# Moving value loads, mixing matrices, a pair of exponentials and row splits in a talking-heads attention with two expert layers

## The chip, the cores and the metric

The kernel runs on one core of a Trainium2 chip. The metric is the device time of one execution in microseconds (us). TensorE (PE) multiplies, VectorE (DVE), ScalarE (ACT) and GpSimd (POOL) work on tiles in SBUF and PSUM, and SyncE (SP) issues the DMAs named here.

## The reference, cut to what matters

```python
def _attn_ref(q, k, v, w_pre, w_post):            # (4, 12, 448, 64)
    scores = scale * np.matmul(q, k.transpose(0, 1, 3, 2))
    scores = np.einsum('bhij,hg->bgij', scores, w_pre)
    scores = scores - np.max(scores, axis=-1, keepdims=True)
    attn = np.exp(scores)
    attn = attn / (np.sum(attn, axis=-1, keepdims=True) + 1e-09)
    attn = np.einsum('bhij,hg->bgij', attn, w_post)
    return np.matmul(attn, v)

def _moe_ref(x, w_in, w_out):                     # x (1792, 768), w_in (768, 2048)
    h = x @ w_in
    g = np.where(h > 0.0, h, np.exp(np.minimum(h, 0.0)) - 1.0)
    return g @ w_out
```

A third layer routes each row of the result to one of eight experts (`x + gate * (relu(x @ w1) @ w2)`, or `x` alone where a skip score is not positive). The change doesn't touch it.

## The kernel before, in words

**Attention.** The 4 batches have 448 query rows each, cut into 4 tiles of 120, 120, 120 and 88 rows, so there are 16 tiles. A tile is worked on in three *periods* of four blocks of 10 query rows (the last tile of a batch has fewer), 48 periods in all, and a period in two *units* of two blocks. The heads are mixed by a matrix product, for which the 12 heads x 10 rows of a block have to lie on the partitions. The scores come out of TensorE with the rows on the partitions (`qk`, L154), ScalarE and VectorE move them from PSUM into one large tile `s` per attention tile (L158, L159), and a DMA per block brings them into a buffer `d` in the other layout (`relayout`, L193). There are two such tiles `s`, used in turn, and eight buffers `d`.

A period n, in the program's order: SP issues the relayout of the second unit of period n+1, the stores of results, and the query and key loads of period n+7. Then, for each of the two units: the first mixing `c` (`mix_pre`, L206, with the matrices `kpre_low` and `kpre_up`); after the first unit's, the relayout of the first unit of period n+2; the second mixing `f` of a unit of period n-1 (`mix_post`, L252); the row maxima `nmx` (`top`, L215, VectorE); two copies of `f` into `at` (L258, one on ScalarE, one on VectorE); and the exponentials `e` (`softmax`, L224, two on ScalarE). After the second unit's exponentials are issued, TensorE computes two heads' pairs of scores for period n+5 (`qk`). Then come the norms (`norm`, L231, L232 on VectorE and L236 on GpSimd), the score moves, the split of queries, and the product of `at` of the previous tile with the values (`av`, L274) and its copy (L283). The PSUM pool `ps_w` has five buffers, shared by `c` and `qk`.

**The order.** Engines run their instructions in the order in which the program issues them; up to the routing tables this order is written by hand. Only behind the point where the tables are made is the order of instructions chosen by a scheduler.

**Start.** Before the first period the program loads queries, keys, the two mixing weights and the 12 pieces of values of batch 0 (`load_v`, L125, on SP), computes all scores of tile 0, issues the relayouts of period 0, builds the mixing matrices (`kron`, L307 and L303 copy them on VectorE, L309 and L311 mask them on GpSimd, DMAs at L357, L359 and L366 put them into their tiles `kpre_low`, `kpre_up` and `kpost`), and issues four pairs of scores of tile 1. Values of the later batches are loaded right after their predecessors' last use, in `av`.

**The second layer.** It starts beside the last five periods of the attention and is a generator, resumed by `next(mix)`. Rows `xr` are loaded (`load_x`, L511), and split into a high part (ScalarE, L515) and a low part (L519, on POOL and VectorE in turn). A weight is loaded as 64-bit words, narrowed to 32 bits (`narrow`: L488 on ScalarE, L491 to L498 on VectorE, and a merge at L500 on POOL), and split in the same way (L463, L464). Six pieces of rows and one weight make one group of products (`products`, L585), 18 matrix multiplications. The groups go through the weights and the four row tiles: weight 0 with row tiles 0, 1, 2, then weight 1 with row tiles 0, 1, 2, then both with row tile 3. The elementwise step follows (`elu`, L592 to L595), and `g` is stored. The second product `o` (L859) reads stored rows back (`gr`, L732) and narrowed weights `wr` (L805).

## Time and profile before

| | us |
|---|---|
| median of 3 runs | 1108.67 |
| lowest and highest run | 1106.9, 1115.65 |
| the profiled execution | 1108.77 |
| its span (first to last instruction) | 1107.0 |
| PE busy | 1024.1 |
| DVE, ACT, POOL busy | 802.3, 566.7, 390.7 |

The span leaves out 1.77 us around it. TensorE's mean granted clock in the profiled execution was 0.981 of full speed. Of the span's 1107.0 us TensorE is busy for 93%. Busy time of other engines matters only where TensorE waits for them.

### The profile page before, as it was taken

How to read it: one execution, taken by the hardware profiler on the slowest of the kernel's cores; microseconds unless marked ns; L12 is line 12 of the kernel's file. 1: busy time of each engine (PE TensorE's matmuls, PEld its weight loads, DVE VectorE, ACT ScalarE, POOL GpSimd, SP SyncE). 2: the span in 40 equal slices, each digit the busy share in tenths (PEclk: the TensorE clock that was granted, in tenths of full speed). 3: DMA queues.
4: the chain of work that ended last, by engine and by line, in shares of the span. 5: the costliest groups of instructions: out<-in, count | busy, mean ns of one | idle time of the engine just before them, and what ended most of it. 6: DMA issues, size and time to landing. Idle time of an engine off the chain costs nothing. (4 is left out here: it accounts for less than half of the span.)

```text
span 1107.0 us, 29935 instructions
## 1 busy us (share of the span) xinstructions
PE 1024.1 (93%) x12082; PEld 882.8 (80%) x12082; DVE 802.3 (72%) x1495; ACT 566.7 (51%) x1150; POOL 390.7 (35%) x355
## 2 busy tenths in 40 slices
PE   6998999899899888999999999999999989899997
PEld 4676667666677667899999988999999978788887
DVE  5775777677577668667666557878787856999953
ACT  5664656466465555444544454333333326677751
POOL 2232214123221226232232202535354534756521
PEclk8999999999999999999999999999999998999999
DMA  6453564465455556555566557733333385999800
GB/s 202 170 173 109 164 202 138 131 195 182 110 165 173 166 153 225 171 170 157 193 215 206 178 171 262 237 94 107 96 105 107 94 317 184 392 391 343 328 8 32
DMA packets 134218, 199.67 MB, mean 180 GB/s; under 512 B 35860, under 2 KB 101400, under 8 KB 133821
## 3 DMA queue, kind: packets, MB, share of 16 engines
q1 hardware_dynamic: 131933, 191.27, 52.4%
q0 software_dynamic: 2144, 6.46, 1.6%
q8 instruction: 96, 1.57, 0.6%
q14 instruction: 45, 0.37, 0.1%
HBM read 122.47 MB, written 37.65 MB: 145 GB/s over the span
## 5 line engine op out<-in xcount | busy, mean ns | idle before, releaser
L859 PE MATMUL o<-w,gh 128*128 128x384 f32 (+2 forms) x1344 | 242.5, 339 | 2.9 <-ACT w L463 2.4
L585 PE MATMUL h<-xh,w 128*128 128x448 f32 x1152 | 236.3, 367 | 4.7 <-POOL xh L519 4.7
L859 PEld LDWEIGHTS o<-w,gh 128*128 128x128 f32 x1344 | 234.1, 190 | 7.3 <-ACT w L463 3.6
L585 PEld LDWEIGHTS h<-xh,w 128*128 128x128 f32 x1152 | 216.9, 189 | 23.4 <-POOL xh L519 6.5
L236 POOL TENSOR_SCALAR kr<-kpost,rs 128x60 f32<-128x60 f32 x180 | 77.4, 444 | 284.5 <-DVE rs L232 242.7
L252 PEld LDWEIGHTS f<-kr,e 64*64 64x64 f32 (+2 forms) x5760 | 121.2, 138 | 54.6 <-issue 33.5
L755 DVE SCALAR_TENSOR_TENSOR junk<-x,wrow 128x768 f32<-128x768 f32 x78 | 117.1, 1501 | 40.0 <-ACT x L890 38.6
L252 PE MATMUL f<-kr,e 64*64 64x60 f32 (+2 forms) x5760 | 122.4, 225 | 7.3 <-DVE at L258 1.8
L500 POOL TENSOR_TENSOR wf<-a,p 128x768 f32<-128x768 f32 x32 | 66.6, 2082 | 163.3 <-DVE p L498 122.8
L215 DVE TENSOR_REDUCE nmx<-c 128x1 f32<-128x448 f32 x180 | 104.5, 620 | 25.9 <-PE c L206 25.9
L258 ACT COPY at<-f 128x480 f32<-128x480 f32 x96 | 52.5, 547 | 135.2 <-PE f L252 135.2
L1029 DVE TENSOR_TENSOR wlo<-w1t,whi 128x1536 fp32r<-128x1536 f32 x50 | 111.6, 2255 | 13.6 <-ACT whi L1026 13.6
L224 ACT ACTIVATE e<-c,nmx 128x448 f32<-128x448 f32 x180 | 113.0, 637 | 6.3 <-DVE nmx L215 6.3
L1026 ACT CAST whi<-w1t 128x1536 fp32r<-128x1536 f32 x64 | 94.3, 1483 | 34.1 <-PE ph L1056 17.5
L748 POOL TENSOR_TENSOR prod<-x,wrow 128x768 f32<-128x768 f32 x39 | 93.9, 2434 | 50.0 <-ACT x L890 26.8
L154 PE MATMUL qk<-k,qq 64*120 64x448 f32 (+1 forms) x576 | 90.6, 404 | 17.3 <-ACT e L224 10.3
L206 PE MATMUL c<-d,kpre_up 60*64 60x448 f32 x336 | 85.1, 574 | 11.7 <-ACT s L158 11.7
L274 PE MATMUL xp<-at,v 128*64 128x120 f32 (+3 forms) x1536 | 92.2, 267 | 1.4 <-DVE at L258 1.4
L274 PEld LDWEIGHTS xp<-at,v 128*64 128x64 f32 (+1 forms) x1536 | 75.1, 137 | 21.9 <-issue 17.3
L159 DVE TENSOR_SCALAR s<-qk 120x448 f32<-120x448 f32 (+1 forms) x96 | 58.3, 618 | 45.0 <-PE qk L154 19.8
L206 PE MATMUL c<-d,kpre_low 64*64 64x448 f32 x336 | 84.3, 554 | 3.5 <-DMA kpre_low<-kpre_kr 3.5
L154 PEld LDWEIGHTS qk<-k,qq 64*120 64x120 f32 (+1 forms) x576 | 52.8, 180 | 42.1 <-ACT e L224 25.2
(185 smaller groups left out, 1449.2 us busy)
## 6 DMA issues: line engine op xcount, KB each, us to landing
w1t<-in_moe_w_dram SPq DMA_DIRECT2D x64, 768.0 KB
d<-s SPq DMA_DIRECT2D x168, 210.0 KB
gT<-g SPq DMA_DIRECT2D x64, 224.0 KB
f<-in_moe_w_in_dram SPq DMA_DIRECT2D x16, 768.0 KB
f<-in_moe_w_out_dram SPq DMA_DIRECT2D x16, 768.0 KB
gr<-gT SPq DMA_DIRECT2D x48, 256.0 KB
rk<-in_k_dram SPq DMA_DIRECT2D x24, 224.0 KB
xr<-xT SPq DMA_DIRECT2D x24, 224.0 KB
```

Of the source, the lines that this page charges most:

```text
L154: nc.tensor.matmul(out=ps[:n, :S], lhsT=qt[T, p // 2][rows, a, p % 2, :n], rhs=kt[b, p][rows, z, :], start=(i == 0), stop=(i == 2))
L206: nc.tensor.matmul(out=ps[j * UP:(j + 1) * UP, :S], lhsT=kpre_up[UP:UP + HP, :] if z else kpre_low if len(U) == 2 else kpre[:d[z, j].shape ...
L215: nc.vector.tensor_reduce(out=t, in_=c, op=ALU.max, axis=AX.X, negate=True)
L224: nc.scalar.activation(out=e, in_=c, func=ACTF.Exp, bias=t, accum_out=sms[U][:, i:i + 1])
L252: nc.tensor.matmul(out=ps[to, c // 2, :, z, :], lhsT=e[rows, keys], rhs=kr[rows, :])
L274: nc.tensor.matmul(out=ps[z * 64:(z + 1) * 64, i, :n], lhsT=t[:, z, jc % t.shape[2], :], rhs=att[T][:t.shape[0], jc, 2 * p + z, :n], start ...
L585: nc.tensor.matmul(out=ps, lhsT=w[:, a, kk, :], rhs=xs[tb, kk][:, z, :], start=(kk == 0 and a + z == 0), stop=(kk == NK - 1 and a == 1))
L748: nc.gpsimd.tensor_tensor(out=p[:, :n], in0=x2, in1=w, op=ALU.mult)
L755: nc.vector.scalar_tensor_tensor(out=t[:, o:o + n], in0=x2, scalar=1.0, in1=w, op0=ALU.mult, op1=ALU.mult, accum_out=lg[:, e:e + 1])
L859: mm = nc.tensor.matmul(out=po[c][:, :cols[c].stop - cols[c].start], lhsT=gs[i][fc // GC][:, a, fc % GC, :], rhs=wo[fc][:, z, cols[c]], st ...
L1026: nc.scalar.copy(out=hi, in_=t)
L1029: (nc.vector if dve else nc.gpsimd).tensor_tensor(out=lo, in0=t, in1=hi, op=ALU.subtract)
```

## The change

Four things are moved or resized:

- The loads of values are collected in a list and issued in the period loop, after the relayout and the stores and ahead of the query loads. Those of batch 0 thus stand in period 0, those of a later batch one period after the product that frees their place.
- In the second unit of a period the two exponentials are issued ahead of the two copies of `f`.
- The mixing matrices are built inside the loop over tile 0's scores, when three of its six pairs have been issued, instead of after the loop and the first relayouts.
- The pool `xr` has nine buffers instead of six, and the six splits of row tile 2 are issued in one piece right after the products of row tile 1, ahead of the narrowing of weight 1.

```diff
--- before.py
+++ after.py
@@ -276,7 +276,7 @@
                                              stop=(i == 1 and jc == JC - 1))
             for p in (2 * u, 2 * u + 1):
                 if b + 1 < B and it == len(ROWS) - 1:
-                    load_v(b + 1, p)
+                    values.append((b + 1, p))
 
             def move():
                 x = x_p.tile([128, 2, 120], FP32, tag="x", name="x")
@@ -284,7 +284,7 @@
                 stores.append((xT[b][2 * u:2 * u + 2, :, r0:r0 + n].rearrange("c p n -> p c n"), x[:, :, :n]))
             return move
 
-        stores = []
+        stores, values = [], []
 
         def store():
             for to, x in stores:
@@ -330,8 +330,7 @@
                 split_k(0, 0, nc.vector)
                 load_k(0, 5)
         load_q(1)
-        for p in range(NK):
-            load_v(0, p)
+        values += [(0, p) for p in range(NK)]
         moves = []
         for p in range(NK):
             if p + 1 < NK:
@@ -342,6 +341,22 @@
             if p > 0:
                 moves.pop()()
             moves.append(move)
+            if p == 2:
+                kpre = kron(pre, "kpre", False)
+                kpost = kron(post, "kpost", True)
+
+                kpre_low = const.tile([UP, UP], FP32, name="kpre_low")
+                nc.vector.memset(kpre_low, 0.0)
+                nc.sync.dma_start(out=kpre_low[GAP:, GAP:], in_=kpre[:HP, :HP])
+                kpre_up = const.tile([128, UP], FP32, name="kpre_up")
+                nc.sync.dma_start(out=kpre_up[UP:UP + HP, :], in_=kpre[:HP, :UP])
+                kposts = [const.tile([128, HP], FP32, name=f"kpost{z}") for z in range(2)]
+                for t in kposts:
+                    nc.vector.memset(t, 0.0)
+                nc.vector.tensor_copy(out=kposts[1][:HP].rearrange("p (g i) -> p g i", g=H),
+                                      in_=kpost[:HP].rearrange("p (g i) -> p g i", g=H)[:, :, :HR])
+                for z, first in ((1, UP), (0, GAP), (0, UP + GAP)):
+                    nc.sync.dma_start(out=kposts[z][first:first + HP, :], in_=kposts[1][:HP, :])
         moves.pop()()
         units = [units_of(Gs) for Gs in periods]
         for U in units[0]:
@@ -349,21 +364,6 @@
         load_q(2)
         split_q(1, 0)
         split_q(1, 1)
-        kpre = kron(pre, "kpre", False)
-        kpost = kron(post, "kpost", True)
-
-        kpre_low = const.tile([UP, UP], FP32, name="kpre_low")
-        nc.vector.memset(kpre_low, 0.0)
-        nc.sync.dma_start(out=kpre_low[GAP:, GAP:], in_=kpre[:HP, :HP])
-        kpre_up = const.tile([128, UP], FP32, name="kpre_up")
-        nc.sync.dma_start(out=kpre_up[UP:UP + HP, :], in_=kpre[:HP, :UP])
-        kposts = [const.tile([128, HP], FP32, name=f"kpost{z}") for z in range(2)]
-        for t in kposts:
-            nc.vector.memset(t, 0.0)
-        nc.vector.tensor_copy(out=kposts[1][:HP].rearrange("p (g i) -> p g i", g=H),
-                              in_=kpost[:HP].rearrange("p (g i) -> p g i", g=H)[:, :, :HR])
-        for z, first in ((1, UP), (0, GAP), (0, UP + GAP)):
-            nc.sync.dma_start(out=kposts[z][first:first + HP, :], in_=kposts[1][:HP, :])
         relayout(units[1][0])
         for i in range(4):
             qk(1, i)()
@@ -383,6 +383,8 @@
             late = n >= NP - 5
             if late:
                 next(mix)
+            while values:
+                load_v(*values.pop(0))
             if T2 < len(tiles):
                 if u2 == 0:
                     load_q(T2)
@@ -396,10 +398,13 @@
                     relayout(units[n + 2][0])
                 moves = mix_post(old[i]) if old else []
                 top(cur[i])
+                if i == 1:
+                    softmax(cur[i])
                 if old:
                     moves[1](nc.scalar.copy)
                     moves[0](nc.vector.tensor_copy)
-                softmax(cur[i])
+                if i == 0:
+                    softmax(cur[i])
                 if i == 1 and T < len(tiles):
                     scores = [qk(T, 2 * u), qk(T, 2 * u + 1)]
                 if late:
@@ -469,7 +474,7 @@
         with ExitStack() as ctx:
             f64_p = pool("f64", 2, ctx, side="right")
             cv_p = pool("cv", 1, ctx, side="right")
-            xr_p = pool("xr", 6, ctx, side="right")
+            xr_p = pool("xr", 9, ctx, side="right")
             xh_p = [pool("xh0", NK, ctx, side="right")]
 
             def load_w(src):
@@ -663,13 +668,12 @@
             xh_p.append(pool("xh3", NK, ctx))
             t_p = pool("tables", 1, ctx)
             ps_o = pool("ps_o", 2, space=PSUM)
-            narrowed[1] = narrow(raws.pop(1))
             raws["out"] = load_w_out(0)
             products(1)
-            split_x(2, range(3), both)
+            split_x(2, range(6), both)
+            narrowed[1] = narrow(raws.pop(1))
             elu(1)
             wi[1] = split(narrowed.pop(1), ring_a)
-            split_x(2, range(3, 6), both)
             load_x(3)
             products(2)
             w_jobs(0)
```

The first place is ScalarE in two periods inside a batch. Numbers tell the buffers apart: `f_2541` is the second mixing's result of a first unit, `f_2592` of a second one. Before:

```order
L258 COPY at_2365<-f_2541 128x48x10
L224 ACTIVATE e_2581,sm_2580<-c_2532,nmx_2574 128x448
L224 ACTIVATE e_2583,sm_2580<-c_2533,nmx_2576 128x448
L258 COPY at_2365<-f_2592 128x48x10
L224 ACTIVATE e_2632,sm_2631<-c_2585,nmx_2625 128x448
L224 ACTIVATE e_2634,sm_2631<-c_2586,nmx_2627 128x448
L158 ACTIVATE s_2462<-qk_2636 120x448
L158 ACTIVATE s_2462<-qk_2644 120x448
L141 CAST qq_2670<-rq_2062 128x240
```

The same in the changed kernel:

```order
L258 COPY at_2365<-f_2541 128x48x10
L224 ACTIVATE e_2581,sm_2580<-c_2532,nmx_2574 128x448
L224 ACTIVATE e_2583,sm_2580<-c_2533,nmx_2576 128x448
L224 ACTIVATE e_2630,sm_2629<-c_2585,nmx_2625 128x448
L224 ACTIVATE e_2632,sm_2629<-c_2586,nmx_2627 128x448
L258 COPY at_2365<-f_2592 128x48x10
L158 ACTIVATE s_2462<-qk_2636 120x448
L158 ACTIVATE s_2462<-qk_2644 120x448
L141 CAST qq_2670<-rq_2062 128x240
```

The copy of `f_2592`, which stood between the two pairs of exponentials, stands behind both.

The second place is SP at the start, from the last of the first query loads on (L112, `rq` of 128x720). Before:

```order
L112 DMA rq<-in_q_dram 128x720
L125 DMA v<-in_v_dram 128x384
L125 DMA v<-in_v_dram 64x128
L193 DMA d_154<-s 120x1x448
L193 DMA d_155<-s 120x1x448
L193 DMA d_156<-s 120x1x448
L193 DMA d_157<-s 120x1x448
L112 DMA rq<-in_q_dram 128x720
L357 DMA kpre_low<-kpre_kr 60x60
L359 DMA kpre_up<-kpre_kr 60x64
L366 DMA kpost_330<-kpost_330 60x60
L366 DMA kpost_329<-kpost_330 60x60 x2
```

Ten more rows of value loads stand between the second and the third row there, like the two shown. In the changed kernel:

```order
L112 DMA rq<-in_q_dram 128x720
L350 DMA kpre_low<-kpre_kr 60x60
L352 DMA kpre_up<-kpre_kr 60x64
L359 DMA kpost_253<-kpost_253 60x60
L359 DMA kpost_252<-kpost_253 60x60 x2
L193 DMA d_154<-s 120x1x448
L193 DMA d_155<-s 120x1x448
L193 DMA d_156<-s 120x1x448
L193 DMA d_157<-s 120x1x448
L112 DMA rq<-in_q_dram 128x720
```

Behind that stand the relayouts of period 1, and the values ahead of the relayouts of period 2 (`d_154` and the following, used again):

```order
L193 DMA d_160<-s 120x1x448
L193 DMA d_161<-s 120x1x448
L125 DMA v<-in_v_dram 128x384
L125 DMA v<-in_v_dram 64x128
L193 DMA d_154<-s 120x1x448
L193 DMA d_155<-s 120x1x448
```

The matrices moved ahead of the first relayouts, and the 12 value loads from ahead of the relayouts of period 0 to behind those of period 1.

The third place is SP about the last groups of the first product, where a scheduler chooses the order (`gr` are row loads, `gT` stores of `g`, `wr` weight loads). Before:

```order
L732 DMA gr<-gT_0_65 128x4x128
L596 DMA gT_3_76<-g 128x448
L732 DMA gr<-gT_0_69 128x4x128
L805 DMA wr<-wf_77 128x768
L805 DMA wr<-wf_78 128x768
L805 DMA wr<-wf_79 128x768
L732 DMA gr<-gT_0_73 128x4x128
L732 DMA gr<-gT_0_61 128x4x128
L805 DMA wr<-wf_80 128x768
L805 DMA wr<-wf_81 128x768
L805 DMA wr<-wf_82 128x768
L732 DMA gr<-gT_0_65 128x4x128
```

In the changed kernel:

```order
L601 DMA gT_1_74<-g 128x448
L809 DMA wr<-wf_77 128x768
L736 DMA gr<-gT_0_73 128x4x128
L809 DMA wr<-wf_78 128x768
L601 DMA gT_2_75<-g 128x448
L809 DMA wr<-wf_79 128x768
L736 DMA gr<-gT_0_61 128x4x128
L736 DMA gr<-gT_0_65 128x4x128
L601 DMA gT_3_76<-g 128x448
L736 DMA gr<-gT_0_69 128x4x128
L809 DMA wr<-wf_80 128x768
L736 DMA gr<-gT_0_73 128x4x128
```

The weight loads `wr` are issued further ahead, the first two between stores, and fewer row loads stand ahead of the last three. On PE, the order of the large products is the same.

## Rows read from the trace of the kernel before

**Rows 1.** the page: busy time and share of each engine, then one of the costliest groups.

```profile
PE 1024.1 (93%) x12082; PEld 882.8 (80%) x12082; DVE 802.3 (72%) x1495; ACT 566.7 (51%) x1150; POOL 390.7 (35%) x355
...
L154 PE MATMUL qk<-k,qq 64*120 64x448 f32 (+1 forms) x576 | 90.6, 404 | 17.3 <-ACT e L224 10.3
```

**Rows 2.** PE waits from 60 to 400 us: us in total, times, longest us.

```profile
PE c L206 <- ACT s L158: 11.7, 3, 4.0
PE qk L154 <- ACT e L224: 9.0, 27, 0.4
```

**Rows 3.** timeline of ACT, 120 to 140 us: start, busy, instruction [idle before <-releaser].

```profile
126.60 0.57 ACT L258 COPY at<-f 128x480 f32<-128x480 f32 x1 [0.29 <-PE f L252]
127.06 0.63 ACT L224 ACTIVATE e<-c,nmx 128x448 f32<-128x448 f32 x1
```

**Rows 4.** timeline of VectorE and of PE, 120 to 140 us.

```profile
125.27 1.16 DVE L215 TENSOR_REDUCE nmx<-c 128x1 f32<-128x448 f32 x2
...
127.84 0.88 PE L154 MATMUL qk<-k,qq 64*120 64x448 f32 x5 [0.32 <-ACT e L224]
128.64 1.50 PE L274 MATMUL xp<-at,v 128*64 128x88 f32 x29
```

**Rows 5.** busy time by stretch, PEclk, DMA share, GB/s (PE, PEld, DVE, ACT, POOL).

```profile
20.00:24.00 4.00, 2.21 (x12) 1.89 (x16) 0.10 (x1) 0.00 (x0) 0.00 (x0) 0.50 0.29 91
108.00:112.00 4.00, 4.00 (x89) 2.80 (x86) 2.99 (x8) 1.66 (x6) 0.43 (x1) 0.57 0.68 206
```

**Rows 6.** timeline of SP (DMA issues) at the start.

```profile
7.45 6.93 SPq L125 DMA_DIRECT2D v<-in_v_dram  x12
14.55 3.56 SPq L193 DMA_DIRECT2D d<-s  x4
18.16 0.49 SPq L112 DMA_DIRECT2D rq<-in_q_dram  x1
...
23.08 10.33 SPq L193 DMA_DIRECT2D d<-s  x12
```

**Rows 7.** timeline of PE at the start: first products of periods 0, 1 and 2.

```profile
21.79 0.97 PE L206 MATMUL c<-d,kpre_low 64*64 64x448 f32 x1 [3.47 <-DMA kpre_low<-kpre_kr]
...
27.61 0.59 PE L206 MATMUL c<-d,kpre_low 64*64 64x448 f32 x1
...
33.96 0.59 PE L206 MATMUL c<-d,kpre_low 64*64 64x448 f32 x1
```

**Rows 8.** timeline of VectorE at the start.

```profile
12.35 1.70 DVE L159 TENSOR_SCALAR s<-qk 120x448 f32<-120x448 f32 x3
...
14.84 0.22 DVE L307 COPY kpre_kr<-pre 120x120 f32<-120x120 f32 x1
...
16.68 0.18 DVE L363 COPY kpost<-kpost_kr 60x60 f32<-60x60 f32 x1 [1.29 <-POOL kpost_kr L311]
...
33.46 1.24 DVE L159 TENSOR_SCALAR s<-qk 120x448 f32<-120x448 f32 x2 [0.65 <-DMA d<-s]
```

**Rows 9.** timeline of POOL, VectorE and PE, 404 to 426 us.

```profile
407.28 4.11 POOL L519 TENSOR_TENSOR xh<-xr,xh 128x448 fp32r<-128x448 f32 x3 [6.19 <-ACT xh L515]
416.28 2.12 POOL L500 TENSOR_TENSOR wf<-a,p 128x768 f32<-128x768 f32 x1 [4.89 <-DVE p L498]
...
407.70 4.17 DVE L519 TENSOR_TENSOR xh<-xr,xh 128x448 fp32r<-128x448 f32 x3 [1.04 <-ACT xh L515]
...
413.07 0.55 DVE L491 TENSOR_SCALAR a<-a 128x768 int32<-128x768 int32 x1
...
419.29 1.01 DVE L464 TENSOR_TENSOR w<-wf,w 128x768 fp32r<-128x768 f32 x1 [2.03 <-ACT w L463]
...
419.54 6.65 PE L585 MATMUL h<-xh,w 128*128 128x448 f32 x23 [4.09 <-POOL xh L519]
```

**Rows 10.** timeline of PE and ACT, 655 to 677 us.

```profile
662.14 8.93 PE L859 MATMUL o<-w,gh 128*128 128x384 f32 x47 [1.90 <-ACT w L463]
...
670.38 0.83 ACT L463 CAST w<-wr 128x768 fp32r<-128x768 f32 x1 [1.72 <-DMA wr<-wf]
```

## The prediction

> **What bounds the kernel now.** I read the page first, then PE's waits, then the timeline at the four places that the change touches: the attention period, the start, the first products of the second layer, and the loads in the middle of its last groups. TensorE is busy for 1024.1 of 1107.0 us [rows 1], so the whole program has about 83 us of PE idle time to win. Where PE runs solid, work on another engine is worth nothing. The reader should look only for idle time in front of a PE instruction and for what released it.
>
> In the attention stretch the large entries are two [rows 2]. Three stalls of 4 us behind the score moves, together 11.7 us, stand at the tile ends of the batches, where the relayouts of short blocks are late; no edit touches them. The other is 27 short waits of the score products for an exponential, 9.0 us together. The page has 10.3 us for that releaser over the whole span [rows 1].
>
> The profiled execution took 1108.77 us, a span of 1107.0 and 1.77 outside it. The median of the runs is 1108.67, so I work from 1108.77 without correction. About 1% (11 us) is what a measurement of this kernel can tell from no change.
>
> **Exponentials ahead of the copy.** In a period ScalarE now does copy, two exponentials, copy, two exponentials. The second copy waits 0.29 us for the mixed values f, starts at 126.60, and the third exponential follows at 127.06 [rows 3]. Its maximum came from two reductions that began at 125.27 and took 1.16 together, so the first was there by about 125.85 [rows 4]. PE waits for just this exponential: 0.32 us, then the rest of the score products from 127.84, and the product with the values at 128.64 [rows 4]. With the pair ahead, the third exponential starts when the second is done (126.60 - 0.29 = 126.31, [rows 3]), 0.75 us earlier. That is more than the 0.32 us wait, which goes. No instruction is added. The displaced copy starts at 126.31 + 2 x 0.62 = 127.55 instead of 126.60 and takes 0.57, so it ends at 128.1; its first reader, the value product in a tile's first period, is due at 128.64 - 0.32 = 128.3. So the cover holds by 0.2 us. What is late next is nothing: PE is continuous across the rest of this period.
>
> Of the 10.3 us I take 9.6, and give 0.3 back for the last periods, where mixture work stands between these steps and the copy feeds the value product at once: **-9.3**. Ends: -10.3 if all goes, -5 if the later copy costs half of it.
>
> **The start.** Two edits meet here. The mixing matrices are now built inside tile 0's scores. PE's first mixing product starts at 21.79 after 3.47 us of waiting for one of them [rows 7], and that wait goes. But the block on VectorE runs from 14.84 to 16.86 (1.29 of it waiting for GpSimd, [rows 8]), about 1.9 us apart from what overlaps, and now stands between two score moves in a strict order. Tile 0's last moves, which ended at 14.05 [rows 8], then end near 16, and the relayouts, issued from 14.55 [rows 6], start near 16.2. The matrices' own transfers fall before that on SP. The first mixing product then comes near 19.5: 16.2 plus 3.3, a bit less than the 3.5 us between the issue end of a relayout (12 from 23.08 in 10.33 us, so the eighth ends at 29.97) and the score move that it frees at 33.46 [rows 6, 8]. That is 2.3 earlier, and period 1, at 27.61 before [rows 7], would start near 24.
>
> The price stands behind that. The 12 value loads took 6.93 us of SP's time while SP had nothing else due [rows 6]. Now they stand after period 0's relayout and ahead of those for period 2. SP's sum: 16.2 + 3.56 (first four relayouts) + 0.5 (one query load) + 4 x 0.86 = 23.7; values to 30.6; the four relayouts of period 2 to 34.0. By the same 3.5 us from issue to use (2.3 to 3.5; the lower from a queue less full) their last one is usable at 36.3 to 37.5, against 33.46 [rows 8]. On it wait the score moves of period 1 (they overwrite the tile that it reads), and these hold the PSUM buffers that period 2's mixing product needs. So period 2, at 33.96 before [rows 7], starts near 37: +3. PE would then have stood idle for some 6 us. After stalls of that kind the granted clock is the lower level: 0.50 in 20 to 24 us behind the 3.47 us wait, and 0.57 in the 4 us after a batch-end stall [rows 5], which costs 0.43 x 4 = 1.7 us where PE is the limit. The clock dip at 20 to 24 us may go in exchange, but what it gives back is lost in the later wait. I take +3 and about +1 for the clock: **+4**. Ends: -1 (the queue is faster than I count and period 2 is ready sooner), +7 (36.3 to 37.5 at its late end plus a full dip and a refill).
>
> For the other batches the value loads move one period on; they stood beside continuous PE work in before, so moving them is worth 0, and -1 to +1 at the ends.
>
> **Rows split ahead of a narrowing.** PE stands 4.09 us, from 415.45 to 419.54, for the lower parts of tile 2's rows [rows 9], because a narrowing (VectorE from 413.07 until the merge on POOL at 416.28, so 3.2, then 2.12 of merge) stood ahead of them. With nine row buffers instead of six, three loads start without waiting for a release, and six splits run before the narrowing. So the products of tile 2 follow at about 415.5 and end near 420, as 23 products took 6.65 and these are 18 [rows 9]. But the next products use the weight that is narrowed behind: splits end near 417 (three beside three took 4.2, [rows 9]), narrowing 3.2 (its first step on ScalarE beside the splits), merge 2.1, and its split into high and low 1.0 on VectorE [rows 9] behind about as much on ScalarE, so the high part at 423.3 and the low part at 424.3. Before, they would start at 419.54 + 18/23 x 6.65 = 424.7. The wait moves from one product to the next, and 424.7 becomes 423.3 to 424.3; of the 0.4 to 1.4 us I take the upper part, as the high part is asked for first: **-1.2**. Ends: -4 (all 4.09), +2.
>
> Here a rule weighs against it. Three splits on POOL took 4.11 us beside three on DVE in 4.17 [rows 9], so as long as six in a row. The Trainium skill, "SBUF — State Buffer", section "SBUF: two separate sides", says that VectorE with two SBUF inputs and GpSimd hold their shared port as an exclusive lock for a whole instruction, so that the other blocks. The trace agrees for these six. By that rule the merge on POOL and VectorE's work beside it run after each other too, the weight comes at 424 or later, and this term would be 0, the sum 1.2 higher.
>
> **The tail of the second layer.** With the loads freed earlier the order gives three weight loads an earlier place on SP, between stores and row loads. PE waits 1.90 us at 662.14 for such a weight, and ScalarE 1.72 for its load at 670.38 [rows 10]. The row loads that they pass become later by an issue of some 0.4 us each. I take **-1.5**; ends -2.8 (all waits there) and +1.
>
> Sum: -9.3 + 4 - 1.2 - 1.5 = -8.0, so 1108.77 - 8.0 = **1100.8 us**.
>
> **Rivals.**
> *Full start.* The queue takes the value loads faster than I count, or the moves need not wait, and the 3.7 us won at period 1 stay. For it: DMA engines are not full at 20 to 24 us (a share of 0.29, [rows 5]). Against it: SP's issue time, not the engines, is my bound. -9.3 - 3.7 - 1.2 - 1.5: 1093.1 us.
> *The exponential's wait was no loss.* PE's ends are modelled, so the 0.3 us gaps may be filled by the next wait, such as the weights or the PSUM buffers. Against: the five products after the gap start only then. With a term of 0, +4 - 2.7: about 1110.1 us; half of it, 1105.
> *Slower: the copy holds the value product.* In the 15 tiles' first periods the value product reads columns which the displaced copy writes. My cover is 0.2 us. If the maximum of the third exponential comes later than I take, ScalarE, in order, holds the copy behind it, and the copy comes up to 1.2 us late (2 x 0.6, [rows 3]); PE waits at the value product with the next mixing products behind it. It decides from the point where the third exponential starts over 0.2 us after the second has ended. Price: 15 x 1.2 = 18 us against the 9.3 won, and with +4 - 2.7 a sum of +10.0: 1118.8 us.
> *The change does not do what it says.* The mixing wait stays, as the weight takes the place of the rows: only the term -1.2 goes, 1102.0 us; that lies within the forecast.
>
> **Chances.** Forecast with its spread (1096 to 1105) 0.54, full start 0.20, no gain from the exponentials 0.18, slower 0.08. The range from 1092 to 1109 leaves out the slower rival and a little below. Faster by over 1% means under 1097.6: the full start (0.20) and the lower quarter of the forecast's spread (0.14) make 0.34. Slower by over 1% (over 1119.8) is most of the slower rival, whose price can be larger where a late copy also delays the mixed values: 0.06. The rest, 0.60, is within 1%.
>
> **What would show it.** Right: the waits of score products for exponentials fall from 27 to a few; the wait for the mixing matrix is gone; a wait of 3 to 6 us stands before period 2 behind a relayout's DMA or the score moves, near 31 to 37 us; the 4.09 us wait at 419.54 is gone and one of 2 to 4 us for the split weight stands in front of the fourth product group; PE after it is solid. Wrong: value products that wait for the ScalarE copy; period 2 that starts before 33; a stall that sits at the batch ends and is longer than 4 us.

## The result and the profile after

The changed kernel took 1097.3 us (median of 4 runs, 1094.9 to 1100.71) against 1111.3 of the kernel before on the same occasion (1106.9 to 1115.65): a ratio of 0.9866, interval 0.9824 to 0.9908. A later comparison of the same two kernels gave 0.9809 (0.9773 to 0.9845). The profiled execution took 1095.63 us with a span of 1093.8, 13.2 less than the span before. The forecast was 1100.8 us and 8.0 less; direction and range held, the gain was larger, and its parts were not those of the sum.

Busy time and the score products' group on the page of the changed kernel, to compare with [rows 1]:

```profile
PE 1020.0 (93%) x12082; PEld 886.1 (81%) x12082; DVE 802.9 (73%) x1496; ACT 563.9 (52%) x1150; POOL 393.2 (36%) x354
...
L154 PE MATMUL qk<-k,qq 64*120 64x448 f32 (+1 forms) x576 | 79.5, 404 | 7.6 <-ACT k L133 5.1
```

The line to read is the second. Idle time ahead of the score products fell from 17.3 to 7.6 us, as forecast, since the part that waited for an exponential is gone. But the group's *busy* time fell too, from 90.6 to 79.5 us, with the same 576 instructions and the same mean. 11.1 us of what the stops cost had been printed as work.

Where the 13.2 us went, from marks in both traces (the first row maximum of a period on VectorE, the first product of a group on TensorE):

| mark | before | after | change since the last mark | forecast |
|---|---|---|---|---|
| first maximum of period 3 | 42.53 | 45.48 | +2.95 | +4 |
| first maximum of period 47 | 392.40 | 379.00 | -16.35 | -9.6 |
| first product of layer 2 | 399.76 | 388.38 | +2.0 | +0.3 |
| fifth group of products | 428.45 | 416.97 | -0.1 | -1.2 |
| 13th group of products | 460.96 | 448.78 | -0.7 | 0 |
| 33rd group of six products `o` | 690.26 | 675.53 | -2.55 | -1.5 |
| 49th group of six products `o` | 710.72 | 697.76 | +1.77 | 0 |
| end of the span | 1107.0 | 1093.8 | -0.2 | 0 |

**The attention period.** A full period, inside a batch, before (timeline of PE, columns as in [rows 3]):

```profile
173.76 1.08 PE L154 MATMUL qk<-k,qq 64*120 64x448 f32 x7
175.16 0.86 PE L154 MATMUL qk<-k,qq 64*120 64x448 f32 x5 [0.32 <-ACT e L224]
175.95 1.90 PE L274 MATMUL xp<-at,v 128*64 128x120 f32 x29
```

And the same period of the changed kernel (timelines of PE and ScalarE; 169.18 is the first exponential of the pair that was moved):

```profile
169.43 1.49 PE L154 MATMUL qk<-k,qq 64*120 64x448 f32 x12
170.85 1.90 PE L274 MATMUL xp<-at,v 128*64 128x120 f32 x29
...
169.18 0.65 ACT L224 ACTIVATE e<-c,nmx 128x448 f32<-128x448 f32 x1
...
170.40 0.59 ACT L258 COPY at<-f 128x480 f32<-128x480 f32 x1
```

The wait has gone, and the 12 score products are one row. From their start to the value product it is 175.95 - 173.76 = 2.19 us before and 170.85 - 169.43 = 1.42 after. So one wait, printed as 0.32, had cost 0.77 us. From mark to mark, full periods went from 7.9 us to 7.1.

In the first period of a tile, though, the moved copy holds the value product, which reads what it writes (ScalarE and PE of the changed kernel):

```profile
49.33 0.59 ACT L258 COPY at<-f 128x480 f32<-128x480 f32 x1
...
49.98 1.90 PE L274 MATMUL xp<-at,v 128*64 128x120 f32 x29 [0.17 <-ACT at L258]
```

The product starts right behind the copy's end. Of the eight full first periods six take 7.34 to 7.38 us instead of 7.11 to 7.15: 0.2 us a tile that the change does not win.

**The start.** SP, PE and VectorE, and two stretches of 4 us (columns as in [rows 5]):

```profile
16.02 3.31 SPq L193 DMA_DIRECT2D d<-s  x4
...
23.24 7.56 SPq L125 DMA_DIRECT2D v<-in_v_dram  x12
30.90 7.08 SPq L193 DMA_DIRECT2D d<-s  x8
...
33.77 1.72 PE L206 MATMUL c<-d,kpre_low 64*64 64x448 f32 x2 [2.69 <-DMA d<-s]
37.04 1.01 PE L206 MATMUL c<-d,kpre_up 60*64 60x448 f32 x1 [1.55 <-ACT s L158]
...
11.95 0.18 DVE L356 COPY kpost<-kpost_kr 60x60 f32<-60x60 f32 x1 [1.29 <-POOL kpost_kr L311]
...
36.48 1.16 DVE L159 TENSOR_SCALAR s<-qk 120x448 f32<-120x448 f32 x2 [5.84 <-DMA d<-s]
...
32.00:36.00 4.00, 1.72 (x2) 0.29 (x2) 0.00 (x0) 0.00 (x0) 0.00 (x0) 0.65 0.59 220
36.00:40.00 4.00, 2.96 (x65) 2.23 (x69) 2.83 (x7) 1.26 (x3) 0.84 (x2) 0.50 0.71 240
```

This went as forecast, nearly to the row. The matrices' block ends at 12.13 inside tile 0's scores, the relayouts are issued from 16.02 (forecast 16.2), the values from 23.24 to 30.80 (23.7 to 30.6), and the score moves of period 1 start at 36.48 (36.3 to 37.5) after 5.84 us of idle time. The first mixing product of period 2 starts at 33.77 and its partner only at 37.04, behind those moves. The granted clock is 0.65 in 32 to 36 us and 0.50 in 36 to 40. Against [rows 7], period 2's first product is no later (33.77 against 33.96), but the others stand still until 37.04, so the period is some 3 us late although period 1 was 2.5 early.

**The first products of layer 2.** PE, POOL, VectorE, and one stretch:

```profile
400.02 7.70 PE L590 MATMUL h<-xh,w 128*128 128x448 f32 x36
411.06 0.68 PE L590 MATMUL h<-xh,w 128*128 128x448 f32 x2 [3.34 <-ACT w L468]
...
408.33 1.81 POOL L505 TENSOR_TENSOR wf<-a,p 128x768 f32<-128x768 f32 x1 [4.15 <-DVE p L503]
...
401.75 3.45 DVE L524 TENSOR_TENSOR xh<-xr,xh 128x448 fp32r<-128x448 f32 x3
405.13 0.55 DVE L496 TENSOR_SCALAR a<-a 128x768 int32<-128x768 int32 x1
...
412.00:416.00 4.00, 3.95 (x12) 3.58 (x13) 3.90 (x6) 2.44 (x5) 0.87 (x1) 0.57 1.02 390
```

The wait of [rows 9] for the rows is gone and one of 3.34 us for the weight stands ahead of the next group, the fourth: VectorE narrows only from 405.13, behind its low parts, and POOL merges at 408.33. Behind the wait the clock is 0.57 in 412 to 416 us, and the fourth group takes 416.97 - 411.06 = 5.91 us where an undisturbed one takes about 3.65. (Of the 0.7 us won behind the fifth group most is a wait for the gate's weights, 1.37 us before and 0.45 after.)

**The tail of the second layer.** PE and ScalarE:

```profile
653.02 0.62 PE L863 MATMUL o<-w,gh 128*128 128x384 f32 x2 [1.19 <-ACT w L468]
...
652.14 1.81 ACT L468 CAST w<-wr 128x768 fp32r<-128x768 f32 x2 [2.08 <-DMA wr<-wf]
```

One wait of 1.19 us for a weight is left of the 1.90 in [rows 10]; the load itself is waited for a little longer (2.08 against 1.72). From the 13th to the 33rd group the change wins 2.55 us. Behind that PE waits for VectorE at the second pair of the routing's small products `pp<-oh`. Before, and then in the changed kernel:

```profile
704.64 0.39 PE L779 MATMUL pp<-oh,upper 128*128 128x8 f32 x2 [1.48 <-DVE oh L776]
...
691.68 0.39 PE L783 MATMUL pp<-oh,upper 128*128 128x8 f32 x2 [3.21 <-DVE oh L780]
```

By the 49th group 1.77 of the 2.55 us are lost again.

**The end of the attention.** The last value products beside layer 2, before (PE and one stretch):

```profile
396.47 0.59 PE L206 MATMUL c<-ds,kpre_kr 48*64 48x448 f32 x1 [2.10 <-DMA ds<-s]
...
397.82 2.01 PE L274 MATMUL xp<-at,v 128*64 128x120 f32 x32
...
396.00:400.00 4.00, 3.53 (x67) 2.89 (x68) 2.07 (x8) 1.47 (x4) 0.59 (x2) 1.00 0.97 311
```

and after:

```profile
383.51 0.59 PE L206 MATMUL c<-ds,kpre_kr 48*64 48x448 f32 x1 [2.09 <-DMA ds<-s]
...
384.88 3.56 PE L274 MATMUL xp<-at,v 128*64 128x120 f32 x32
...
384.00:388.00 4.00, 4.00 (x57) 3.37 (x54) 1.95 (x7) 1.47 (x4) 1.24 (x3) 0.60 0.98 346
```

The same 32 products take 2.01 and 3.56 us. Ahead of both stands a wait for a relayout of nearly one length (2.10 us before, 2.09 after), but only after one of them was the clock down, at 0.60. That is 1.55 of the +2.0 us here. It need not come from the edits: one and the same program (values in front, below) took 7.35 us from the first maximum of period 47 to layer 2 in one profile and 10.34 in another.

### The profile page after: what moved, and what is told of

Read it like the earlier page. It is cut to its first block, busy times and chain, and to the rows that moved or that the text cites. A ratio compares the mean times of both kernels' runs of the same rounds, so it can differ in the third digit from the quotient of the medians.

```text
span 1093.8 us, 29911 instructions
## 1 busy us (share of the span) xinstructions
PE 1020.0 (93%) x12082; PEld 886.1 (81%) x12082; DVE 802.9 (73%) x1496; ACT 563.9 (52%) x1150; POOL 393.2 (36%) x354
## 3 DMA queue, kind: packets, MB, share of 16 engines
q8 instruction: 96, 1.57, 0.6%
## 5 line engine op out<-in xcount | busy, mean ns | idle before, releaser
L236 POOL TENSOR_SCALAR kr<-kpost,rs 128x60 f32<-128x60 f32 x180 | 80.4, 461 | 273.9 <-DVE rs L232 211.7
L252 PEld LDWEIGHTS f<-kr,e 64*64 64x64 f32 (+2 forms) x5760 | 123.4, 139 | 57.3 <-issue 40.0
L252 PE MATMUL f<-kr,e 64*64 64x60 f32 (+2 forms) x5760 | 126.0, 226 | 7.8 <-issue 3.9
L206 PE MATMUL c<-d,kpre_up 60*64 60x448 f32 x336 | 85.5, 572 | 13.2 <-ACT s L158 13.2
L206 PE MATMUL c<-d,kpre_low 64*64 64x448 f32 x336 | 87.6, 552 | 2.7 <-DMA d<-s 2.7
L154 PE MATMUL qk<-k,qq 64*120 64x448 f32 (+1 forms) x576 | 79.5, 404 | 7.6 <-ACT k L133 5.1
L258 DVE COPY at<-f 128x480 f32<-128x480 f32 x96 | 59.6, 621 | 19.0 <-PE f L252 16.0
```

Source lines behind the costliest of these rows:

```text
L206: nc.tensor.matmul(out=ps[j * UP:(j + 1) * UP, :S], lhsT=kpre_up[UP:UP + HP, :] if z else kpre_low if len(U) == 2 else kpre[:d[z, j].shape ...
L252: nc.tensor.matmul(out=ps[to, c // 2, :, z, :], lhsT=e[rows, keys], rhs=kr[rows, :])
L258: copy(out=to[:, :, r + j * k:r + (j + 1) * k], in_=at[:, :, :k])
```

## The experiments

Totals are compared with the kernel before, run beside each on the same chip.

### Which edit brings the gain, and by how much a place

Theory P: a stop in a row of products costs more than the idle time that is printed for it. Theory S: each is worth its printed 0.3 us and something else brought the rest.

**Exponentials alone.** Of the change only this is made in the kernel before:

```diff
+                if i == 1:
+                    softmax(cur[i])
                 if old:
                     moves[1](nc.scalar.copy)
                     moves[0](nc.vector.tensor_copy)
-                softmax(cur[i])
+                if i == 0:
+                    softmax(cur[i])
```

> Only the pair of exponentials is moved ahead of the copies. Theory P (a stopped row of score products costs more than the idle time that the profile prints: 12 products took 2.26 us with the stop and 1.49 without): period 3 starts where it did before (first maximum at 42.5), and the stretch from period 3 to period 47 is 16 to 19 us shorter than before, in all 16 to 19 us off the kernel before. Theory S (each wait is worth its 0.3 us and the rest of the gain comes from the values' loads that left the periods): 9 to 10 us off that stretch and off the whole.

Measured: 1094.49 us against 1111.09, ratio 0.9842 (0.9803 to 0.9881), 16.6 us less. From period 3 to period 47 it is 16.2 us shorter. The page's row of this run:

```profile
L154 PE MATMUL qk<-k,qq 64*120 64x448 f32 (+1 forms) x576 | 79.3, 407 | 5.7 <-ACT k L133 4.9
```

So this one edit brings most of the gain of the change (14.0 us, and 21.5 when it was repeated), and theory S falls: with the values' loads where they were, the busy time of the score products falls as in the changed kernel. (Period 3 itself came at 41.37, 1.1 earlier than P said, since periods 1 and 2 hold two of the places.)

**Every other period.**

```diff
-                if i == 1:
+                if i == 1 and n % 2 == 0:
                     softmax(cur[i])
 ...
-                if i == 0:
+                if i == 0 or n % 2:
                     softmax(cur[i])
```

> The kernel before with the pair of exponentials ahead of the copies in every other period only. If each stopped row of score products costs its own 0.77 us, full periods alternate between 7.1 and 7.9 us and the stretch from period 3 to period 47 is 8 to 9 us shorter than before. If a saved wait is given back in the next period, the pace is 7.9 or 7.5 in all and the saving is under 4 us. By 0.3 us a place it would be 4 to 5 us.

Measured: 1101.64 us against 1114.12, ratio 0.9896 (0.9834 to 0.9958), and 10.0 us less from period 3 to period 47. Full periods alternate, 7.11 and 7.9 us. Two neighbours, PE's timeline:

```profile
162.36 1.45 PE L154 MATMUL qk<-k,qq 64*88 64x448 f32 x12
163.74 1.90 PE L274 MATMUL xp<-at,v 128*64 128x120 f32 x29
...
169.47 1.06 PE L154 MATMUL qk<-k,qq 64*120 64x448 f32 x7
170.87 0.87 PE L154 MATMUL qk<-k,qq 64*120 64x448 f32 x5 [0.34 <-ACT e L224]
171.66 1.04 PE L274 MATMUL xp<-at,v 128*64 128x120 f32 x16
```

Unbroken, 163.74 - 162.36 = 1.38 us from the first score product to the value product; stopped, 171.66 - 169.47 = 2.19. The remaining waits of this run, 60 to 395 us:

```profile
PE qk L154 <- ACT e L224: 4.5, 13, 0.4
```

A little under half of the waits is left and a little over half of the gain is there. The price belongs to each place; nothing is given back in the next period.

**One exponential ahead.** In the kernel with the values in front (below), of the pair only the first goes ahead (`softmax` has got a second argument, which of the two it issues; that part is not shown):

```diff
                 if i == 1:
-                    softmax(cur[i])
+                    softmax(cur[i], (0,))
 ...
-                if i == 0:
-                    softmax(cur[i])
+                softmax(cur[i], (0, 1) if i == 0 else (1,))
```

> As the run with the values in front, but of the second pair only the first exponential stands ahead of the copies, and the other behind them. If only that exponential is waited for (it frees the one PSUM buffer that the fourth group of score products needs), the full periods keep their 7.1 us and the time is that of the run with the values in front within what clock dips scatter. If the second exponential of the pair or the place of the copy sets the pace, the periods go back to 7.4 to 7.9 us, 8 to 20 us longer in all.

Measured: 1092.09 us against 1114.12, ratio 0.9819 (0.9752 to 0.9885); full periods take 7.11 to 7.15 us. ScalarE and PE in one:

```profile
128.80 0.64 ACT L226 ACTIVATE e<-c,nmx 128x448 f32<-128x448 f32 x1
...
129.67 0.57 ACT L262 COPY at<-f 128x480 f32<-128x480 f32 x1
130.13 0.64 ACT L226 ACTIVATE e<-c,nmx 128x448 f32<-128x448 f32 x1
...
129.56 1.47 PE L154 MATMUL qk<-k,qq 64*120 64x448 f32 x12
130.97 1.13 PE L278 MATMUL xp<-at,v 128*64 128x88 f32 x24
```

The products run in one row although the second exponential of the pair (130.13) starts 0.6 us after the first of them. Only the first one was waited for. The copy comes 0.87 us after the start of the pair's first exponential (129.67 - 128.80) instead of 1.22 (170.40 - 169.18), and that shows in the first periods of the tiles: 7.12 to 7.15 us in five of the eight full ones, against 7.34 to 7.38 in six of the changed kernel's. In the time as a whole it is lost in the scatter.

### The start

**Both edits of the start undone** in the changed kernel (values loaded ahead of the scores, matrices built behind them):

```diff
-        values += [(0, p) for p in range(NK)]
+        for p in range(NK):
+            load_v(0, p)
 ...
-            if p == 2:
-                kpre = kron(pre, "kpre", False)
 ...
+        kpre = kron(pre, "kpre", False)
 ...
```

> The changed kernel with batch 0's values and the mixing matrices back at their old places at the start. If the values ahead of period 2's relayouts cost 3 us net, period 3's first maximum comes at 42.5 instead of 45.5 and the time is about 3 us below the changed kernel's. If the start of the change is neutral (what it loses at period 2 it saves in later periods), the time is the changed kernel's within 1 us.

Measured: 1089.3 us against 1111.09, ratio 0.9791 (0.9741 to 0.984). Period 3's maximum comes at 42.85, 2.6 us before that of the changed kernel.

**Values in front, matrices early.**

```diff
-        values += [(0, p) for p in range(NK)]
+        for p in range(NK):
+            load_v(0, p)
```

> The changed kernel with batch 0's values loaded at the front again, the mixing matrices still early. If SP's order alone delays period 2, then period 1's maximum stays near 26.4, period 2's comes near 32.5, period 3's near 39.5, and the time is 5 to 6 us below the changed kernel's. If the values' transfers crowd out the first relayouts when they run early, the first mixing product comes after 22 and the gain over the changed kernel is under 3 us.

Measured: 1091.33 us against 1111.09, ratio 0.9821 (0.9774 to 0.9867). The stage times missed what was expected: maxima of periods 1, 2 and 3 at 29.58, 36.00 and 41.99. SP and PE:

```profile
7.44 7.21 SPq L125 DMA_DIRECT2D v<-in_v_dram  x12
14.76 0.88 SPq L351 DMA_DIRECT2D kpre_low<-kpre_kr  x1
...
19.16 3.31 SPq L193 DMA_DIRECT2D d<-s  x4
...
22.04 0.56 PE L206 MATMUL c<-d,kpre_low 64*64 64x448 f32 x1 [1.29 <-DMA d<-s]
```

The values are issued until 14.65 with nothing else held up, but the five issues for the matrices now stand between them and the relayouts, which start at 19.16 instead of 16.02 (and 14.55 in [rows 6]). The first mixing product waits for them until 22.04. So the early matrices gain nothing with the values in front: both edits of the start are tied by SP's order.

**Values one period later**, behind the relayouts of period 2:

```diff
-            while values:
+            while values and n > 0:
                 load_v(*values.pop(0))
```

> The changed kernel with batch 0's values one period later, behind all relayouts of period 2 and ahead of period 3's. If the values' place in SP's queue ahead of period 2's relayouts is what holds period 2, its maxima come near 33 and period 3's near 39.5 to 40.5, and the time is 5 to 6 us below the changed kernel's. If the values' transfers are dear wherever they run among relayouts, period 3's come after 42.

Measured: 1087.65 us against 1114.12, ratio 0.9764 (0.9701 to 0.9828). Period 2's maximum comes at 33.46 and period 3's at 40.34, 5.1 us before the changed kernel's and 2.2 before that of the kernel before. SP and PE:

```profile
19.80 6.84 SPq L193 DMA_DIRECT2D d<-s  x8
26.69 8.70 SPq L125 DMA_DIRECT2D v<-in_v_dram  x12
...
32.35 0.59 PE L206 MATMUL c<-d,kpre_up 60*64 60x448 f32 x1 [0.71 <-ACT s L158]
```

The relayouts of period 2 are issued as part of the eight from 19.80, the values stand behind them, and of the 2.69 and 1.55 us of waiting at period 2 there is 0.71 left. This is the order that the change would have needed at the start.

**Later batches' values where they were.** In the kernel with the values in front:

```diff
-                    values.append((b + 1, p))
+                    load_v(b + 1, p)
```

> As the run with the values in front, with the later batches' values too issued where the kernel before has them, right behind the products that free their place. If those loads lie beside continuous TensorE work in both orders, periods 13 to 16 and the time are those of the run with the values in front, within 2 us. If the order in those periods pays, periods 13 to 16 are 0.5 us or more longer each, 4 to 6 us over three batches.

Measured: 1091.28 us against 1112.44, ratio 0.9798 (0.9764 to 0.9833). The maxima of periods 13 to 16 come 6.67, 6.71, 6.96 and 7.35 us after the one before, against 6.67, 6.73, 7.06 and 7.35 with the loads moved. Moving those loads is worth nothing, as the forecast had it.

### The first products of layer 2

**Mixing undone** in the changed kernel (six row buffers, the narrowing ahead of the splits):

```diff
-            xr_p = pool("xr", 9, ctx, side="right")
+            xr_p = pool("xr", 6, ctx, side="right")
 ...
+            narrowed[1] = narrow(raws.pop(1))
 ...
-            split_x(2, range(6), both)
-            narrowed[1] = narrow(raws.pop(1))
+            split_x(2, range(3), both)
 ...
+            split_x(2, range(3, 6), both)
```

> The changed kernel with six row buffers and the narrowing ahead of the splits again. If the wait only moved from the rows to the weight, the fifth group of products starts at the same distance from the second as in the changed kernel (16.9 us, within 0.4) and the time is equal within 1 us. If the reorder is worth its first wait less a part of the second, that distance is 1.5 to 4 us longer.

Measured: 1096.97 us against 1111.09, ratio 0.9865 (0.9802 to 0.9928), like the changed kernel's. From the second to the fifth group it is 17.1 us; the changed kernel has 16.95 and the kernel before 17.11. PE:

```profile
407.82 14.54 PE L590 MATMUL h<-xh,w 128*128 128x448 f32 x62 [4.03 <-POOL xh L524]
```

The wait of 4.03 us for the rows is back, the one for the weight is gone, and the sum is the same within 0.2 us. Further on the edit does show. The tail has the old waits again: from the first product `o` to its 33rd group this run takes 41.5 us and the changed kernel 37.5, and from there to the 49th 18.9 against 22.2. And the run with both edits of the start undone differs from that with the exponentials alone only in this edit and in the place of the later values, which was worth nothing above; it took 1089.3 us and the other 1094.49 on the same occasion.

**Rows between.** In the kernel with the values in front, VectorE narrows after its first low part, and POOL merges after its three:

```diff
-            split_x(2, range(6), both)
-            narrowed[1] = narrow(raws.pop(1))
+            step = narrowing(raws.pop(1))
 ...
+            low_x(2, 0, nc.gpsimd)
+            low_x(2, 1)
+            next(step)
 ...
+            low_x(2, 2, nc.gpsimd)
+            low_x(2, 4, nc.gpsimd)
+            next(step)
+            next(step)
+            narrowed[1] = next(step)
+            low_x(2, 3)
+            low_x(2, 5)
```

> As the run with the values in front, with the narrowing of weight 1 on VectorE put behind the first low part of row tile 2 and ahead of the others, and its merge behind POOL's three low parts. If two waits compete for VectorE's order, the distance from the second to the fifth group of products falls from 16.9 us to about 14.6 and the time by 2 us. If the port shared by VectorE and POOL makes the steps run after each other in any order, the distance stays above 16.

Measured: 1090.63 us against 1114.12, ratio 0.979 (0.9724 to 0.9856). The distance from the second to the fifth group is 14.75 us, as expected of two waits that compete for VectorE's order. The longest wait left inside this stretch is 1.72 us. But PE then stops again further on:

```profile
402.40 1.48 PE L591 MATMUL h<-xh,w 128*128 128x448 f32 x6 [1.72 <-DVE xh L525]
...
420.60 1.49 PE L591 MATMUL h<-xh,w 128*128 128x448 f32 x6 [1.57 <-POOL xh L525]
```

From the second to the 13th group it is 48.5 us, against 48.4 with the values in front and 48.8 in the changed kernel. The wait moved once more, to the rows of tile 3 (1.57 us at 420.60).

### The totals side by side

The changed kernel and two of the other starts were run again on one chip, with no edit beyond those shown.

> The changed kernel itself, on one chip with the three that follow, to compare the totals: 13 to 15 us below the kernel before, with period 2's stall of 4 us again.

Measured: 1090.90 us against 1112.44, ratio 0.9809 (0.9773 to 0.9845), 21.5 us less and so more than expected.

> Values in front again: if the start is worth what the first look's stage times say, 4 to 7 us below the changed kernel; if that look was a lucky one for the clock, within 2 us.

Measured: 1091.54 us, ratio 0.9801 (0.9766 to 0.9836).

> Values behind period 2's relayouts again: 5 us below the changed kernel at period 3 and 4 to 8 us below it in all.

Measured: 1091.02 us, ratio 0.9794 (0.9758 to 0.983), not the 4 to 8 us below the changed kernel that were expected.

The marks are near those of the earlier profiles (within 0.1, 1.6 and 0.7 us): period 3's first maximum at 45.54, 43.53 and 39.72 us, so 2.0 and 5.8 us apart from the changed kernel. Of the 5.8, 3.5 are there at period 45 (361.07 and 357.58) and 3.2 at the 33rd group of six products `o` (674.05 and 670.83). In the totals nothing is left. What takes these 3.2 us is the clock: from there to the 49th group the run with the values in period 1 took 23.4 us and the changed kernel 20.0, with a granted clock of 0.71 and 0.50 in the two stretches of 4 us from 684 us on in the one and 1.00 there in the other. It is scatter: the earlier profile of the same program took 19.7 us there, with a clock of 1.00. The run with the values in front loses its 2.0 us in another way, in the same 957 products of layer 2. It comes first here, then the changed kernel:

```profile
440.58 197.83 PE L591 MATMUL h<-xh,w 128*128 128x448 f32 x957
...
443.63 193.77 PE L590 MATMUL h<-xh,w 128*128 128x448 f32 x957
```

Neither row has a printed gap, and the granted clock is 1.00 in both from 444 to 636 us. Two other profiles (one exponential ahead, rows between) have the slower pace in this stretch too, 3.72 us for a group of 18 instead of 3.64; what sets it is open. So the start's price is shown at its place, and open in the total: the totals of single programs scatter by 3 to 13 us, the differences sought are 3 to 6.

## Why the prediction was right or wrong

**The exponentials: right in mechanism, mis-sized.** The step that failed is "of the 10.3 us I take 9.6": it priced 31 waits at the idle time that the profile prints. The waits did go. But a stop costs 0.77 us, not 0.32. The page shows both halves, 9.7 us of idle and 11.1 us of busy time less. Part of the wait lies inside the printed time of the last product before the stop: twelve unbroken products start 0.118 us apart (1.42 / 12), so the eighth was due 0.83 us after the first and came 1.40 after it (175.16 - 173.76). The rest is in the restart: five products need 0.79 us to the next instruction instead of 0.59. In place of -9.6, the stretch gave -16.35 in the changed kernel and -16.2 alone. 29 of the 31 places lie in it, and 29 x 0.77 would be 22.3. Part of what lacks is the clock: (1 - granted clock) times the length of the stretch is 12.0 us against 8.5 before (period 36's maximum came 9.78 us after the one before it, against 8.19). In the four profiles with the values in front where it was 8.5 again, the stretch was 18.8 to 22.3 us shorter than before. Another part is idle time ahead of the products `f`, 4.7 us between 60 and 400 us against 3.0. The rest is not settled in its parts.

The same mis-sizing spoiled the copy's cover. With 0.77 us off, the value product is due at 128.64 - 0.77 = 127.9, and not 0.2 us behind the copy's end at 128.1 but 0.2 ahead of it; 0.2 us is what the first periods of the tiles are longer by.

**The start: right.** +4 was forecast, +2.95 came, by the steps as they stood: the late moves, SP's sum, the last relayout, the moves that overwrite its tile, the PSUM buffers behind them. At period 2 the loss was 3.64 us (first maxima at 35.24 and 38.88), and that period's unbroken row of score products gave 0.7 back. The +1 for the clock did not come: summed up to period 3, 4 x (1 - granted clock) is 3.4 us in both kernels, since the dip at 20 to 28 us went and the one at 32 to 40 came. From issue to use the relayout that decides took 2.0 us (the fourth of the eight from 30.90 ends near 34.4, the moves start at 36.48); for the 2.3 at the lower end of the forecast no row was shown. The runs with another place for the values show that it is SP's order that costs this, and that the loss is of the change's own making.

**Rows ahead of the narrowing: the wait moved, and its price with it.** -1.2 was forecast, -0.1 measured at the fifth group, and with the edit undone the distance to it is the same within 0.2 us. The forecast had the new wait right (2 to 4 us for the weight; 3.34 came), and the fourth group did start earlier, 11.04 us after the second instead of 13.47. But the forecast charged the lower clock to the old wait alone; the new one has it too, and the fourth group took 5.91 us instead of 3.64. The sum by the rule of the Trainium skill ("SBUF — State Buffer", section "SBUF: two separate sides") that the prediction cites, 0 for this term, came nearer, but not in the way that the prediction had drawn from it: the weight was not late, and beside POOL's merge (408.33 to 410.14) VectorE had nothing to do from 408.79 on. In another order of the same steps the distance fell by 2 us, which the rule as I used it excluded, and the wait came back further on. From the second to the 13th group the four profiles with the old order (the kernel before, exponentials alone, every other period, mixing undone) have 49.2 to 51.8 us, that of rows between 48.5, and the nine others 48.4 to 49.1. So the order mostly chooses where PE waits, and 0.1 us or more is won by the 13th group; how much is open.

**The tail: right at its place, and partly lost behind it.** -1.5 was forecast; -2.55 came up to the 33rd group, and the longer wait for the routing's products, which the forecast did not have, took 1.77 of it. From the first product `o` to the 33rd group the ten profiles with the new order have 35.4 to 37.5 us and the four with the old one 39.7 to 41.5; from there to the 49th they have 19.7 to 23.4 and 18.9 to 20.5.

**The rivals.** The full start did not come. "No gain from the exponentials" was the opposite of what happened: the modelled ends hid a larger loss, not a smaller one. The slower rival was right that the copy holds the value product in the tiles' first periods, but by 0.2 us and not 1.2. The whole came out 5 us below the forecast on the profiled pair, because the one mis-sized term was 7 us too small, while the mixing stage and the end of the attention gave back 2.8 more than was counted.

## What to carry to other kernels

Price a stop in a row of matrix products by comparing two rows, a stopped and an unbroken one, from their first start to the start of what follows; here the printed idle time is less than half of it, and the group's busy time held the rest. Where such a stop goes, whatever was just in time behind it can become the next wait, as the copy did. Before loads are moved back in an in-order issue queue, ask what then stands behind them and what that overwrites: here twelve issues of 0.6 us delayed relayouts whose source was due to be overwritten, and one place further back they no longer did. Where two engines' work bounds a stage, an edit of its order moves the wait, so look two or three groups further on before counting the gain.

## What the runs showed of the hardware that had not been expected

The granted clock falls after like waits in some executions and not in others (0.60 and 1.00 behind waits of 2.09 and 2.10 us above). Summed over stretches of 4 us in the first 760 us, 4 x (1 - granted clock) is 15.4 us in the profiled execution of the kernel before, 22.3 in that of the changed kernel, and 12.0 and 18.9 in two of one same kernel (values in front), whose spans were 1081.0 and 1090.3 us. The scatter of the totals is of that size. The slower pace of the same 957 products at a granted clock of 1.00 (197.83 and 193.77 us above) adds 4 us in some executions. The changed kernel thus gained 13.2 us in an execution with more half-clock time than the one it was compared with. That may be part of why the repeated comparison gave 21.5, but no more than a part: the repeat's own profile has 20.6.
